# A two-layer attention and MLP kernel: pairwise LayerNorm rstd, zeroing and warming by TensorE, split weight loads, activations stored with chunks innermost, and an offset table for the planner

## Chip, cores, metric

The kernel runs on one core of a Trainium2 chip (trn2). Times are device microseconds of that core. A comparison uses fast runs only, and a ratio is of runs made on the same chip in the same rounds (e1, the last run, has one run of the kernel before of its own; the other seven are those of the runs d1 to d4, on the same chip). Runs whose labels start with a, b and c were made on three different chips, d and e on a fourth, so where ratios of different letters are set side by side, each was taken against the kernel before on its own chip.

The granted clock is the share of TensorE's full clock that its throttle let through; 1.00 is full speed. PE is the matmul engine (TensorE), PEld its weight loads, DVE VectorE, ACT ScalarE, POOL GpSimd, SP the engine that issues DMAs.

## The reference, cut

```python
# x: 1 x 2048 x 512 bf16.  Two layers, each:
x = x + A(layernorm(x))     # 32 heads of 16, causal window of 256, projections wqkv and wo
x = x + B(layernorm(x))     # gelu(x @ w1 + b1) @ w2 + b2, hidden size 1792
def _layernorm(x, eps=1e-5):
    return (x - mean(x)) / sqrt(var(x) + eps)
```

## The kernel before

A planner inside the kernel schedules its operations by list scheduling, with a priority and an estimated duration for each, and emits one fixed order for each engine. Semaphores hold the dependences. An engine can come to stand at an operation whose input is late: in d1, below, DVE stood 4.80 us at a copy whose input had not landed, with other work behind it. An operation may have an alternative engine, and the planner chooses at its planned time.

LayerNorm of a tile of 128 tokens gives `xn` (tokens on partitions). PE transposes its four 128-column chunks to PSUM (the memory that PE writes its results to), and DVE or ACT copies the transposed tile to `xnTA` (for Q, K, V) or `xnTB` (for the MLP). Q, K and W1 read those as the moving operand (the one that streams through the array), V as the stationary one (the weights).

```python
xnTA = sb("xnTA", [P, 2, DC, 2 * P])        # P = 128, DC = 4: chunk, then token
xnTB = sb("xnTB", [P, 2, DC, 4 * P])
...                                         # start
for h in range(2):                          # DVE zeroes PSUM
    add("dve", lambda e, B, h=h: e.memset(ps[:, 4 * h : 4 * h + 4, :], 0.0), 2200, ...)
...                                         # layernorm(tau, layer, dst, dcol, dname, prio), for one tile
add("dve", ... e.bn_stats(...) ...); add("dve", ... e.bn_aggr(...) ...)
add("pool", ... veps = var + EPS, 215, ...); add("pool", ... rstd = pow(veps, -0.5), 590, ...)
add("dve", lambda e, B: e.tensor_scalar(out=xn[:, s, :], in0=X[:, t, :], scalar1=mean, scalar2=rstd,
    op0=ALU.subtract, op1=ALU.mult), 310, ...)
add("pe", tr, 4 * 56.0, ...)                # four transposes to PSUM
evac(lambda B: dst[:, :, dcol : dcol + P],  # DVE or ACT: tokens adjoin in memory
     lambda B: psb[:, B[g][0], 0 : DC * P].rearrange("p (c q) -> p c q", c=DC), 512, ...)
...                                         # uses
(Wqkv_sb[:, dc, ...], xnTA[:, xs, dc, :], ...)                     # Q, K: stationary, moving
(xnTA[:, xs, dc, j * P : (j + 1) * P], Wqkv_sb[:, dc, 2 * D : 3 * D], ...)   # V
(W1_sb[:, dc, fc * P : (fc + 1) * P], xnTB[:, js, dc, 0:M], ...)   # W1, M = 512 or 256
```

The softmax here doesn't subtract the row's maximum and nothing guards it: scores larger than these inputs give would overflow.

## Time and profile before

The median was 534.04 us in the first three runs.

| | before |
|---|---|
| span of the profiled run | 535.7 us |
| PE, ACT, DVE, POOL busy | 472.1, 427.4, 387.3, 292.4 us |
| first exponential | 20.64 us |
| 20 W1 matmuls of 512 columns in a row | 4.49 us |

The page's first part, of the kernel before:

```profile
span 535.7 us, 19845 instructions
## 1 busy us (share of the span) xinstructions
PE 472.1 (88%) x8944; PEld 254.8 (48%) x8944; DVE 387.3 (72%) x739; ACT 427.4 (80%) x514; POOL 292.4 (55%) x376
```

Busy time in windows, kernel before. Each line is a stretch, its length, busy time and instructions of PE, PEld, DVE, ACT and POOL, then granted clock, DMA share and GB/s:

```profile
0.00:20.00 20.00, 9.50 (x68) 6.60 (x68) 13.07 (x25) 5.46 (x8) 10.74 (x46) 1.00 0.94 313
20.00:80.00 60.00, 45.29 (x1100) 26.65 (x1100) 49.22 (x99) 51.04 (x60) 40.28 (x52) 0.89 0.18 46
80.00:500.00 420.00, 385.05 (x7511) 201.63 (x7510) 313.98 (x596) 357.67 (x418) 235.92 (x273) 0.96 0.06 14
```

Groups of instructions, kernel before (output and inputs, shapes, count, then busy us and mean ns of one, then idle before it):

```profile
L585 PE MATMUL ps<-xnTB,W_sb 128*128 128x512 bf16 x336 | 82.1, 385 | 4.7 <-ACT gT L829 2.3 <-DVE gT L817 0.9 <-DVE xnTA L538 0.6
...
L585 PE MATMUL ps<-xnTA,Wqkv_sb 128*128 128x256 bf16 x512 | 71.4, 283 | 8.8 <-DVE KT L629 2.7 <-ACT E L704 1.9 <-ACT QT L540 1.4
...
L561 DVE TENSOR_SCALAR xn<-X,statmv,rstd 128x512 bf16<-128x512 bf16 x64 | 41.5, 653 | 2.7 <-POOL rstd L558 2.5
...
L540 ACT ACTIVATE xnTB<-ps 128x512 bf16<-128x512 bf16 x14 | 8.4, 613 | 1.6 <-PE ps L569 1.4
...
L538 DVE COPY xnTB<-ps 128x512 bf16<-128x512 bf16 x18 | 7.5, 422 | 7.0 <-PE ps L569 6.9
```

### The profile page before, as it was taken

The numbers are of one execution on the slowest core, as the hardware profiler recorded it, in microseconds if no ns is written. First come the engines' busy times: TensorE is split into PE (matmuls) and PEld (weight loads), VectorE is DVE, ScalarE is ACT, GpSimd is POOL, SyncE is SP. The second block draws the span as 40 slices with busy tenths as digits, with TensorE's granted clock in tenths as the row PEclk, the third lists the DMA queues.
The fourth block names the chain that finished last, engine by engine and source line by source line (L and its number), as shares of the span: only waits on it lengthen the run. The fifth ranks groups of instructions, "written<-read, shape, count | busy, mean of one in ns | idle before, by whom it ended". The sixth has DMA issues, their size and how long they took to land.

```text
span 535.7 us, 19845 instructions
## 1 busy us (share of the span) xinstructions
PE 472.1 (88%) x8944; PEld 254.8 (48%) x8944; DVE 387.3 (72%) x739; ACT 427.4 (80%) x514; POOL 292.4 (55%) x376
## 2 busy tenths in 40 slices
PE   3886688998979999599999879998999879989997
PEld 2543455555544545345444444444544444444563
DVE  5996878496979578775899588884878648793531
ACT  2689779888987988979888988689876888699552
POOL 6576746274684457452588347860585425871410
PEclk9997979999979999689999999999999989999999
DMA  8910001010100001000000011000110001100000
GB/s 277 325 42 23 2 4 23 1 25 1 24 2 13 12 3 23 4 1 22 14 13 3 2 23 23 2 4 6 33 29 21 2 8 39 42 2 4 29 21 29
DMA packets 16020, 15.82 MB, mean 30 GB/s; under 512 B 3264, under 2 KB 15424, under 8 KB 15936
## 3 DMA queue, kind: packets, MB, share of 16 engines
q1 hardware_dynamic: 15936, 14.56, 9.5%
q8 instruction: 70, 1.15, 0.9%
q14 instruction: 14, 0.11, 0.1%
HBM read 8.00 MB, written 2.10 MB: 19 GB/s over the span
## 4 chain that ended last, share of the span: by engine, by line
PE 60%; DVE 18%; ACT 18%; issue 2%; POOL 2%; POOLq 0%; DVEq 0%
PE ps L585 46%; ACT E L704 12%; PE ps L737 6%; PE ps L691 6%; DVE KT L629 3%; DVE xn L561 2%; DVE stat L551 2%; ACT gT L820 2%; DVE E L715 2%; PE ps L569 2%; DVE OD L747 2%; DVE gT L817 1%; ACT L820 1%; DVE X L841 1%; DVE X L594 1%
## 5 line engine op out<-in xcount | busy, mean ns | idle before, releaser
L704 ACT ACTIVATE E<-ps 128x1024 bf16<-128x1024 f32 x320 | 305.5, 1037 | 58.8 <-PE ps L691 58.1
L718 POOL TENSOR_TENSOR E<-E,mask 128x512 bf16<-128x512 bf16 x151 | 177.3, 1182 | 143.4 <-ACT E L704 143.1
L585 PE MATMUL ps<-xnTB,W_sb 128*128 128x512 bf16 (+1 forms) x560 | 116.8, 347 | 5.1 <-ACT gT L829 2.3
L585 PE MATMUL ps<-W_sb,gT 128*128 128x512 bf16 x448 | 114.9, 380 | 0.3 <-DVE X L841 0.3
L715 DVE TENSOR_TENSOR E<-E,mask 128x512 bf16<-128x512 bf16 x105 | 66.0, 632 | 27.0 <-ACT E L704 26.8
L691 PE MATMUL ps<-QT,KT 32*64 32x320 bf16 (+4 forms) x3072 | 70.2, 267 | 14.8 <-ACT E L704 8.5
L585 PE MATMUL ps<-xnTA,Wqkv_sb 128*128 128x256 bf16 x512 | 71.4, 283 | 8.8 <-DVE KT L629 2.7
L585 PEld LDWEIGHTS ps<-xnTB,W_sb 128*128 128x128 bf16 x560 | 51.9, 101 | 49.4 <-issue 3.9
L691 PEld LDWEIGHTS ps<-QT,KT 32*64 32x64 bf16 x3072 | 34.3, 105 | 68.6 <-ACT E L704 33.5
L829 ACT ACTIVATE gT<-ps,b1T 128x512 bf16<-128x512 f32 (+1 forms) x92 | 50.2, 584 | 18.0 <-PE ps L585 17.7
L837 POOL TENSOR_TENSOR Xb<-X,b2all 128x512 f32<-128x512 bf16 x32 | 37.7, 1179 | 44.3 <-DVE X L841 29.8
L585 PEld LDWEIGHTS ps<-W_sb,gT 128*128 128x128 bf16 x448 | 39.9, 98 | 41.6 <-issue 3.6
L585 PEld LDWEIGHTS ps<-xnTA,Wqkv_sb 128*128 128x128 bf16 x512 | 46.6, 101 | 25.3 <-DVE KT L629 4.1
L747 DVE STREAM_TRANSPOSE OD<-ps 128x512 f32<-128x512 f32 x64 | 45.4, 710 | 17.2 <-PE ps L737 15.7
L737 PE MATMUL ps<-E,Va 64*17 64x64 bf16 (+3 forms) x1920 | 51.0, 240 | 5.8 <-ACT E L704 3.0
L737 PEld LDWEIGHTS ps<-E,Va 64*17 64x17 bf16 x1920 | 40.8, 89 | 27.9 <-issue 16.8
L737 PE MATMUL ps<-E,Vs 64*17 64x64 bf16 (+3 forms) x1920 | 51.7, 240 | 0.0
L629 DVE TENSOR_TENSOR KT<-ps,parmask 128x1024 bf16<-128x1024 f32 x32 | 38.4, 1208 | 17.7 <-PE ps L585 17.3
L841 DVE TENSOR_TENSOR X<-Xb,ps 128x512 bf16<-128x512 f32 x32 | 21.8, 681 | 34.1 <-PE ps L585 33.9
L569 PE MATMUL ps<-ident,xn 128*128 128x128 bf16 x256 | 25.9, 230 | 20.3 <-DVE xn L561 9.8
L561 DVE TENSOR_SCALAR xn<-X,statmv,rstd 128x512 bf16<-128x512 bf16 x64 | 41.5, 653 | 2.7 <-POOL rstd L558 2.5
L551 DVE BATCH_NORM_STATS2 stat<-X 128x6 f32<-128x512 bf16 x64 | 42.2, 665 | 0.4
(45 smaller groups left out, 481.7 us busy)
## 6 DMA issues: line engine op xcount, KB each, us to landing
Vs<-Va SPq DMA_DIRECT2D x64, 68.0 KB, 2.0
W_sb<-in_B_w_dram SPq DMA_DIRECT2D x2, 1792.0 KB, 14.8
out_dram<-X SPq DMA_DIRECT2D x16, 128.0 KB, 1.7
Wqkv_sb<-in_A_wqkv_dram SPq DMA_DIRECT2D x3, 512.0 KB, 7.0
X<-in_A_x_dram SPq DMA_DIRECT2D x1, 1024.0 KB, 10.4
X<-in_A_x_dram SPq DMA_DIRECT2D x2, 256.0 KB, 3.0
X<-in_A_x_dram SPq DMA_DIRECT2D x1, 512.0 KB, 8.4
Wo_sb<-in_A_wo_dram SPq DMA_DIRECT2D x1, 512.0 KB, 9.4
```

The source lines that it names most:

```text
L551: add("dve", lambda e, B: e.bn_stats(stat6[:, k6, :], X[:, t, :]), 680, reads=["X%d" % t], writes=["st%d" % k6], prio=prio)
L561: add("dve", lambda e, B: e.tensor_scalar(out=xn[:, s, :], in0=X[:, t, :], scalar1=statmv[:, k, 0:1], scalar2=rstd[:, k : k + 1], op0=ALU. ...
L585: r = e.matmul(ps[:, B[g][0], cols], lhsT, rhs, start=st, stop=sp)
L629: add("dve", lambda e, B, g=g, i=i: e.tensor_tensor(out=KT[:, kb, :, 2 * i : 2 * i + 2, :].rearrange("p a c q -> p a (c q)"), in0=ps[:, B[ ...
L691: x = e.matmul(ps[HK * par : HK * par + HK, bk[r], o : o + n], KT[rows, kb, par, c, m * HK : m * HK + HK], QT[rows, c, q : q + n], start=T ...
L704: a = (add("act", lambda e, B, g_=g_, gi=gi: e.activation(E[:, 2 * gi : 2 * gi + 2, e0 : e0 + 512], ps[:, B[g_][0] : B[g_][0] + 2, :], AF. ...
L715: add("dve", lambda e, B: e.tensor_tensor(out=Ew, in0=Ew, in1=Mw, op=ALU.mult), 355 * n, reads=["E%d%s" % (es, x) for es in ess for x in " ...
L718: alt=(("pool", lambda e, B: e.tensor_tensor(out=Ew, in0=Ew, in1=Mw, op=ALU.mult), POOL_M * n, POOL_H, True),))
L737: x = e.matmul(ps[32 * r : 32 * r + VW, B[g][par], q_lo * HK : q_hi * HK], V[rows, (2 * b + m // 2) % VR, c * HC + 2 * r + par, :], E[rows ...
L747: add("dve", lambda e, B: e.transpose(OD[:, s, :], ps[:, B[g][0] : B[g][0] + 2, 0 : 2 * P]), 715, reads=["ps:" + g], writes=["OD%d" % s], ...
L829: gelu_last[0] = add("act", lambda e, B, g=g, fc=fc: e.activation(gT[:, fc, 0:M], ps[:, B[g][0], 0:M], AF.Gelu_apprx_tanh, bias=b1T[:, fc ...
L837: add("pool", lambda e, B, t=tau % T, xs=xs: e.tensor_tensor(out=Xb[:, xs, :], in0=X[:, t, :], in1=b2all[:], op=ALU.add), 1180, reads=["X% ...
```

## The change

The intent is to start sooner, to take work off POOL and to fill PE's gaps with a better order:
- LayerNorm's rstd for two tiles at once, the add of eps on POOL or DVE, the normalisation on DVE or POOL.
- PSUM is zeroed by 18 zero matmuls, which also warm PE; the parity mask is made by three operations instead of 16 selects.
- Q and K weights are loaded in halves.
- Transposed activations are stored token first, the four chunks innermost.
- `_TUNE` holds an offset to the priority of nearly every operation, and a second one for its alternative engine, the outcome of a search. Planned durations are set anew.

```diff
+_TUNE = { "ln": [-704, -709, -762, ...], ... }     # [cut: 2584 numbers under 36 keys]
 def add(..., key=None, more=False):
+    if key in self.tune: prio += self.tune[key][j]   # [cut: counting j; alternatives take key + "*"]
-        xnTA = sb("xnTA", [P, 2, DC, 2 * P])
-        xnTB = sb("xnTB", [P, 2, DC, 4 * P])
+        xnTA = sb("xnTA", [P, 2, 2 * P, DC])
+        xnTB = sb("xnTB", [P, 2, 4 * P, DC])
-        for h in range(2):
-            add("dve", lambda e, B, h=h: e.memset(ps[:, 4 * h : 4 * h + 4, :], 0.0), 2200, ...)
+        for h in range(NWARM):                          # NWARM = 18
+            add("pe", lambda e, B, bk=bk: e.matmul(ps[:, bk, :], gT[:, 0, 0:P], gT[:, 0, :], ...), mm(512), ...)
+        load_w(0, 0, D // 2, ...); load_w(1, 0, D // 2, ...)   # [cut] Q and K in halves, then V
+            add("pool", addeps, 215, ..., alt=(("dve", addeps, 105, 0.0, False),))
+            add("pool", ... rstd[:, k : k + 2] = pow(rstd[:, k : k + 2], -0.5), 580, ...)
-            add("dve", <normalise>, 310, ...)
+            add("dve", norm, 395, ..., alt=(("pool", norm, POOL_XN, 0.0, True),))   # POOL_XN = 620.0
-            evac(lambda B: dst[:, :, dcol : dcol + P],
+            evac(lambda B: dst[:, dcol : dcol + P, :].rearrange("p q c -> p c q"),
-  xnTA[:, xs, dc, :]    xnTA[:, xs, dc, j * P : (j + 1) * P]    xnTB[:, js, dc, 0:M]
+  xnTA[:, xs, :, dc]    xnTA[:, xs, j * P : (j + 1) * P, dc]    xnTB[:, js, 0:M, dc]
```

## The prediction

> **What bounds the kernel now.** No engine alone. The page: PE 472.1 us busy of 535.7 (88%), ACT 427.4 (80%), DVE 387.3, POOL 292.4. The chain of waits is 60% PE, 18% ACT, 18% DVE: engines with fixed orders wait for each other in short pieces. By stretch (busy time in windows):
> - 0 to 20 us: PE 9.5 us busy; first transpose at 8.3 us, first projection at 10.5, first exponential at 20.6.
> - 20 to 80: PE 45.3, ACT 51.0 of 60, granted clock 0.89; no MLP work yet.
> - 80 to 500: PE 385 of 420 (35 us idle), clock 0.96.
> - 500 to 536: PE 32.2 of 36; the last 28 W2 matmuls run at 222 ns each.
>
> PE idles 63 us in all, and granted clock lost about 4% (some 22 us). The wait list gives PE's idle time to many releasers of 1 to 10 us each: poor ordering, not one slow operation. ACT waits 58 us for scores.
>
> **What the change does.**
> 1. *Start.* Two DVE memsets of PSUM (1.76 us each, until 5.19) go; the first statistics started at 5.11 although X was issued at 0.79 and landed about 3.0 us later: up to 1 us gained. 18 zero matmuls warm PE: the first 16 projection matmuls took 3.19 us, later groups of 16 took 1.91, so about 1.3 us.  Waiting for both tiles' statistics costs about 0.8 us. Half-size weight loads let K start earlier. Net 3 to 5 us.
> 2. *Paired rstd.* 64 pow (596 ns) and 64 add-eps (252 ns) become 32 each: about 27 us off POOL. Perhaps 1 to 3 us of time. POOL may now take normalisations, and DVE's mean of 653 ns for them (median 414, longest 1345) shows port waits that better placement can cut.
> 3. *Chunks innermost.* The evacuation writes with an 8-byte step. The Trainium skill, "VectorE: DVE Perf Modes", Mode 2×_1P, asks for unit step; so I expect DVE's copies of transposes to go from about 0.41 us to about 0.68 us (what its fp32 casts of this shape take): about 10 us more DVE work over 38 copies, mostly hidden. Matmuls read with the 8-byte step: two elements per 16-byte line, which "SBUF — State Buffer", the cachelines note under Door 1, gives as enough for full bandwidth. I expect W1 and projection matmul durations unchanged (379 and 273 ns). No trace shows that yet.
> 4. *Offset table.* Reorders every engine and reassigns alternatives. This is the main term: I expect it to remove about half of the 35 us idle in the middle plus part of the lost clock (20 to 24 us), and 4 to 6 us of 20 to 80.
>
> PE's work is unchanged, so busy time with full clock (about 450 us) plus start and drain is a floor near 470.
>
> **Prediction: 506 us**, 8 in 10 within 489 to 523. Faster by over 2%: 0.88; within 2%: 0.09; slower: 0.03.
>
> **What would show it.** First exponential by 16 to 17 us; PE busy share over 91%; clock at least 0.97; PE idle from 80 us on under 20 us; ACT waiting under 40 us for scores; POOL pow x32 at about 580 ns; transposes' DVE copies about 0.68 us.
>
> **What would make it wrong.** Strided moving or stationary reads slowing PE (durations of W1 and projection groups rise); a table tuned to planned durations that the chip doesn't keep, so idle moves instead of going; slower evacuations on the chain; warm-up lost because PE idles again.

## More of the kernel before

The mean of a matmul is its latency (385 ns for 512 columns), and neighbours overlap. What a matmul costs a busy PE is its spacing, which the timeline shows where a run of equal matmuls is unbroken. Here, 20 of 512 columns take 4.49 us, 225 ns each. That stretch runs to the end of the last one; from start to start it is (4.49 - 0.385) / 19 us, or 216 ns:

```profile
237.25 4.49 PE L585 MATMUL ps<-xnTB,W_sb 128*128 128x512 bf16 x20
```

## The result and the profile after

The changed kernel took 686.5 us (median of 4) against 534.75 for the kernel before: ratio 1.2837, interval 1.2806 to 1.2869. It is 28% slower where 5% faster was predicted.

The page's first part, changed kernel:

```profile
span 684.2 us, 19714 instructions
## 1 busy us (share of the span) xinstructions
PE 613.4 (90%) x8864; PEld 270.8 (40%) x8962; DVE 411.4 (60%) x753; ACT 439.5 (64%) x498; POOL 330.2 (48%) x299
```

The span grew by 148.5 us and PE's busy time by 141.3. PE's idle time grew by only 7 us, and PE's share of the span rose from 88% to 90%. By itself a high share says little; here it says that the same work takes PE longer.

Windows, changed kernel:

```profile
0.00:20.00 20.00, 16.39 (x70) 7.53 (x71) 9.45 (x25) 7.96 (x8) 12.05 (x24) 1.00 0.92 317
20.00:80.00 60.00, 49.43 (x865) 23.74 (x867) 38.60 (x68) 43.38 (x47) 35.40 (x30) 0.91 0.16 44
80.00:500.00 420.00, 381.07 (x5790) 168.16 (x5856) 274.23 (x499) 280.67 (x313) 219.10 (x192) 0.98 0.04 10
```

Between 80 and 500 us PE is as busy as before (381 against 385 us), at a slightly higher granted clock (0.98), and gets through 5790 instructions instead of 7511. The groups say which:

```profile
L841 PE MATMUL ps<-xnTB,W_sb 128*128 128x512 bf16 x316 | 152.8, 629 | 12.2 <-issue 5.1 <-DVE xnTB L779 2.9 <-ACT xnTB L781 2.3
...
L841 PE MATMUL ps<-xnTA,Wqkv_sb 128*128 128x256 bf16 x512 | 128.0, 404 | 5.6 <-ACT xnTA L781 1.8 <-DVE xnTA L779 1.6 <-ACT xnTB L781 0.7
...
L841 PE MATMUL ps<-W_sb,gT 128*128 128x512 bf16 x408 | 105.0, 381 | 5.8 <-issue 3.3 <-DVE xnTB L779 1.0 <-ACT gT L1076 0.6
...
L814 POOL TENSOR_SCALAR xn<-X,statmv,rstd 128x512 bf16<-128x512 bf16 x37 | 78.6, 2128 | 12.8 <-PE ps L825 10.8
...
L779 DVE COPY xnTB<-ps 128x512 bf16<-128x512 bf16 x23 | 29.8, 1303 | 29.4 <-PE ps L825 29.3
...
L781 ACT ACTIVATE xnTB<-ps 128x512 bf16<-128x512 bf16 x9 | 11.8, 1310 | 10.0 <-PE ps L825 10.0
```

Matmuls that stream `xnTA` or `xnTB` went from 385 to 629 ns and from 283 to 404; those of W2, which stream `W_sb`, stayed at 381. (Some records of matmuls are missing: 316 and 408 stand for 336 and 448.) The copies of transposes tripled on DVE and doubled on ACT. A normalisation on POOL, planned at 620 ns, takes 2128. The spacing, from the timeline of the changed kernel, to hold against 4.49 us:

```profile
295.91 9.20 PE L841 MATMUL ps<-xnTB,W_sb 128*128 128x512 bf16 x20
```

That is 460 ns a matmul instead of 225 (from start to start, 451 instead of 216). For 256 columns the timelines show 16 in 3.79 us after (237 ns each) and 14 in 1.70 us before (121). An estimate of the cost is 336 x 235 ns + (224 + 512) x 116 ns = 164 us, enough for the whole loss. It has three rivals: the slow copies, the offset table with its mis-planned normalisations, and both.

### The profile page after: what moved, and what is told of

Read it like the earlier page. It is cut to its first block, busy times and chain, and to the rows that moved or that the text cites. A ratio compares the mean times of both kernels' runs of the same rounds, so it can differ in the third digit from the quotient of the medians.

```text
span 684.2 us, 19714 instructions
## 1 busy us (share of the span) xinstructions
PE 613.4 (90%) x8864; PEld 270.8 (40%) x8962; DVE 411.4 (60%) x753; ACT 439.5 (64%) x498; POOL 330.2 (48%) x299
## 4 chain that ended last, share of the span: by engine, by line
PE 77%; DVE 13%; ACT 5%; issue 3%; POOL 1%; POOLq 0%
PE ps L841 63%; PE ps L947 6%; PE ps L993 5%; DVE xnTA L779 2%; ACT E L960 2%; DVE xnTB L779 1%; ACT xnTA L781 1%; PE ps L825 1%; DVE KT L885 1%; DVE OD L1003 1%; ACT xnTB L781 1%; PE ps L738 1%; DVE X L851 1%; DVE E L971 1%; DVE stat L791 1%
## 5 line engine op out<-in xcount | busy, mean ns | idle before, releaser
L960 ACT ACTIVATE E<-ps 128x1024 bf16<-128x1024 f32 x320 | 308.7, 1030 | 121.8 <-PE ps L947 121.6
L974 POOL TENSOR_TENSOR E<-E,mask 128x512 bf16<-128x512 bf16 x144 | 169.6, 1184 | 146.9 <-ACT E L960 146.6
L841 PE MATMUL ps<-xnTB,W_sb 128*128 128x512 bf16 (+1 forms) x540 | 208.2, 536 | 13.2 <-issue 5.2
L841 PE MATMUL ps<-xnTA,Wqkv_sb 128*128 128x256 bf16 x512 | 128.0, 404 | 5.6 <-ACT xnTA L781 1.8
L841 PE MATMUL ps<-W_sb,gT 128*128 128x512 bf16 x408 | 105.0, 381 | 5.8 <-issue 3.3
L841 PEld LDWEIGHTS ps<-xnTB,W_sb 128*128 128x128 bf16 x560 | 58.7, 111 | 110.5 <-issue 71.3
L814 POOL TENSOR_SCALAR xn<-X,statmv,rstd 128x512 bf16<-128x512 bf16 x37 | 78.6, 2128 | 12.8 <-PE ps L825 10.8
L947 PE MATMUL ps<-QT,KT 32*64 32x320 bf16 (+4 forms) x3072 | 70.6, 268 | 14.4 <-ACT E L960 7.6
L841 PEld LDWEIGHTS ps<-xnTA,Wqkv_sb 128*128 128x128 bf16 x512 | 53.3, 112 | 62.3 <-issue 7.7
L1073 DVE TENSOR_SCALAR gT<-ps,b1T 128x512 bf16<-128x512 f32 (+1 forms) x48 | 32.7, 682 | 40.7 <-PE ps L841 40.6
L779 DVE COPY xnTB<-ps 128x512 bf16<-128x512 bf16 x23 | 29.8, 1303 | 29.4 <-PE ps L825 29.3
```

Source lines behind the costliest of these rows:

```text
L779: return add("dve", lambda e, B: e.tensor_copy(dst(B), src(B)), 410 if two else d_psum(n), reads=reads, writes=writes + ([] if free else r ...
L814: return e.tensor_scalar(out=xn[:, s, :], in0=X[:, t, :], scalar1=statmv[:, k, 0:1], scalar2=rstd[:, k : k + 1], op0=ALU.subtract, op1=ALU ...
L841: r = e.matmul(ps[:, B[g][0], cols], lhsT, rhs, start=st, stop=sp)
L947: x = e.matmul(ps[HK * par : HK * par + HK, bk[r], o : o + n], KT[rows, kb, par, c, m * HK : m * HK + HK], QT[rows, c, q : q + n], start=T ...
L960: a = (add("act", lambda e, B, g_=g_, gi=gi: e.activation(E[:, 2 * gi : 2 * gi + 2, e0 : e0 + 512], ps[:, B[g_][0] : B[g_][0] + 2, :], AF. ...
L974: alt=(("pool", lambda e, B: e.tensor_tensor(out=Ew, in0=Ew, in1=Mw, op=ALU.mult), POOL_M * n, POOL_H, True),))
```

## The experiments

### The layout, taken out and put in

*a1_after_old_layout*: the change with the old layout, with the same order on every engine.

```diff
-        xnTA = sb("xnTA", [P, 2, 2 * P, DC])     # xnTB, its writes and its reads likewise
+        xnTA = sb("xnTA", [P, 2, DC, 2 * P])
```

> The whole change, but with the transposed activations in the layout of before (chunk outermost, tokens contiguous); the order on every engine is the same as in the changed kernel. Theory L (the layout costs the time): matmuls on these activations return to spacings of about 216 ns (512 columns) and 108 ns (256), copies of transposes to about 410 ns on DVE and 600 on ACT, and the time falls from 686 to 505 to 525 us, below before (534). Rival O (the offset table made an order for durations the chip does not keep, above all normalisations planned at 620 ns on POOL and measured at 2083): the time stays above 600 us.

Measured: 523.4 us, ratio to before 0.9754 (0.9693 to 0.9816), matmuls back at 380 and 279 ns. Rival O falls as a cause of the loss: the same order that took 686 us is now 2.5% faster than before. By the interval it is faster, though not surely by 2%.

*a2_before_new_layout*: the kernel before with the new layout alone.

> The kernel before with only the layout changed to chunks innermost, order unchanged. Theory L: 680 to 705 us (534 plus about 167 us of PE streaming: 336 matmuls at +239 ns, 224 and 512 at about +117, with little absorbed). Rival O: below 570 us.

Measured: 701.5 us, ratio 1.3074 (1.3007 to 1.3142). So the layout accounts for the whole loss, and the rest of the change is a gain.

### Reading or writing

In both, the plan is that of the kernel before. Their outputs are wrong, which doesn't matter for the times.

```diff
 # a3_before_read_strided: written as before, read with the 8-byte step
-    xnTB[:, js, dc, 0:M]
+    flat(xnTB)[0 : 4 * M].rearrange("p (q c) -> p c q", c=DC)[:, dc]
 # a4_before_write_strided: written with the 8-byte step, read as before
-    evac(lambda B: dst[:, :, dcol : dcol + P], ...)
+    evac(lambda B: flat(dst)[0 : 4 * M].rearrange("p (q c) -> p c q", c=DC)[:, :, dcol : dcol + P], ...)
```

> The kernel before; activations are written contiguous as before, but the matmuls read them with the 8-byte step (wrong results on purpose). Theory L with the matmul read as its cause: 670 to 700 us, copies of transposes unchanged at about 410 and 600 ns. Rival E (the slow strided evacuation copies, 1300 ns on DVE and ACT, sit on the chain and cost most of it): below 570 us.

> The kernel before; activations are written with the 8-byte step, but the matmuls read contiguous (wrong results on purpose). Theory L with the matmul read as its cause: 540 to 560 us, only the copies at about 1300 ns show (about 34 us more DVE and 18 us more ACT work, partly hidden). Rival E: above 620 us.

Measured: reading alone 676.6 us, ratio 1.2613 (1.2550 to 1.2676); writing alone 568.0 us, ratio 1.0593 (1.0529 to 1.0657). Both expectations named the right side, but writing cost more than the 540 to 560 us given. Together (1.3074) they cost almost the sum, 26.1% and 5.9%. In the groups of the strided writes (a4), the copies are slow:

```profile
L567 DVE COPY xnTB<-ps 128x512 bf16<-128x512 bf16 x18 | 23.2, 1302 | 8.8 <-PE ps L598 8.7
...
L569 ACT ACTIVATE xnTB<-ps 128x512 bf16<-128x512 bf16 x14 | 18.3, 1336 | 3.5 <-PE ps L598 3.5
```

Of the 164 us estimated for reading, 139 (676.6 less the 537.7 of before in those rounds) show in the time: PE's busy time grew by 154 us (472.1 to 626.2), and its idle time shrank by 15. The strided copies add latency between a transpose and the matmuls that wait for it. PE's waits for these copies, all lines together, are 4.9 us in the kernel before and 24.5 us in a4. That is 20 of the 30 us that it lost, although neither DVE (72% busy) nor ACT (79%) is full. One of these lines, projections that wait for a copy on DVE, in the kernel before and in a4 (us in total, times, longest):

```profile
PE ps L585 <- DVE xnTA L538: 0.6, 2, 0.3
```

```profile
PE ps L614 <- DVE xnTA L567: 8.5, 12, 1.2
```

### Which step is slow

*b1_before_pairs_innermost* stores two chunks innermost, so the step is 4 bytes. *b2_before_read_16byte_step* reads the layout with chunks innermost as even tokens, then odd ones.

```diff
+    flat.rearrange("p (h q t) -> p h t q", h=2, t=2)      # b1: 4-byte step, written and read, result right
+    flat.rearrange("p (b a c) -> p c a b", a=2, c=DC)     # b2: 16-byte step in Q, K, W1 reads, result wrong
```

> The kernel before with two chunks innermost, so that the matmuls read every second element (a 4-byte step[...]) and the evacuations write with that step; results stay right. Theory S (the moving operand streams at full rate only where neighbouring elements adjoin): spacing of the 512-column matmuls about 450 ns as with the 8-byte step, time near 700 us. Rival C (the rate [...]falls off at some step): spacing about 216 ns, time below 575 us.

> The kernel before with chunks innermost, where the matmuls read even tokens first and then odd ones, so with a 16-byte step[...] (wrong results on purpose). Theory S (only adjoining elements stream at full rate, otherwise one element per slow cycle): same spacing as with the 8-byte step, about 455 ns, time 695 to 710 us. Rival C[...]: about 900 ns, time above 850 us.

Measured in one look each: 547.4 and 1070.1 us. The timeline lines of the two, in that order:

```profile
240.94 4.69 PE L614 MATMUL ps<-xnTB,W_sb 128*128 128x512 bf16 x20
```

```profile
445.89 18.16 PE L614 MATMUL ps<-xnTB,W_sb 128*128 128x512 bf16 x20
```

| step between elements | 2 B | 4 B | 8 B | 16 B |
|---|---|---|---|---|
| 20 matmuls of 512 columns, us | 4.49 | 4.69 | 9.20 | 18.16 |
| ns each | 225 | 235 | 460 | 908 |
| ns from start to start | 216 | 226 | 451 | 899 |
| granted clock in that stretch | 1.00 | 1.00 | 1.00 | 0.50 |
| DVE copy with that step in the write, median ns | 424 | 735 | 1307 | not tried |
| ACT copy likewise, median ns | 597 | 748 | 1308 | not tried |

Rival C holds. Theory S expected 450 ns at 4 bytes, and it got 235. But the 16-byte stretch ran at a granted clock of 0.50 (the mean of b2 is 0.67), and a stretch at 450 ns slowed to half by the clock would look the same. The trace of b2 settles it. In a stretch at full clock the matmuls are just as far apart, (5.56 - 1.08) / 5 us, or 896 ns. The stretch at full clock, then the windows of it and of the 18.16 us:

```profile
430.66 5.56 PE L614 MATMUL ps<-xnTB,W_sb 128*128 128x512 bf16 x6
```

```profile
430.66:436.00 5.34, 5.34 (x14) 0.57 (x6) 2.66 (x5) 1.94 (x2) 1.98 (x2) 1.00 0.01 3
446.00:464.00 18.00, 18.00 (x22) 2.56 (x22) 3.32 (x7) 3.38 (x4) 0.79 (x2) 0.50 0.00 1
```

The 8-byte step doesn't follow the clock either: in the changed kernel 18 matmuls of 256 columns took 4.24 us (from 153.55 us on) at a mean granted clock of 0.60, and 16 took 3.79 us at 1.00, 226 ns from start to start in both. Without a step the clock counts: in the kernel before, 15 took 3.27 us at 0.54, and 14 took 1.70 us at 1.00.

So in these runs a moving operand of bf16 streams at nearly full rate at a step of 4 bytes, and at a rate that halves with each further doubling, whatever the granted clock. That b2 was granted so little clock, though PE was busy for 93% of its span, is not explained by any run. As a stationary operand the 8-byte step is cheap: in the changed kernel V's weight loads took 117 ns on average instead of 97, and V's matmuls kept a median of 379 ns. (Even that rise need not be the step's: loads of W1's weights, whose layout did not change, rose from 101 to 111 ns.) What in the memory makes it so no run here shows.

### What the rest of the change brought

The prediction gave the whole change 28 us and let the layout cost next to nothing; the rest brought 2.5%, some 13 us. These runs use the old layout.

```diff
 # b3_oldlayout_norm_on_DVE
-    add("dve", norm, 395, ..., alt=(("pool", norm, POOL_XN, 0.0, True),))
+    add("dve", norm, 395, ...)
 # b4_oldlayout_norm_DVE_no_offsets: b3 and, as c3_oldlayout_no_offsets without b3:
-    }, _TUNE)
+    }, {})
```

> The whole change with the old layout, and with the normalisation never given to POOL (27 of 64 were on DVE, 37 on POOL at 2.1 us each against a planned 0.62). Theory N (that mis-sized alternative eats the expected gain: PE waited 11 us for it, and 16 us of weight-load waits): 508 to 516 us, against 523 with it. Rival T (the order itself is what stays short of the gain): 519 to 528 us.

> As the run before it (old layout, normalisation on DVE), with every offset of the table at zero. If the table is the main term of the gain, as predicted: 528 to 540 us. If the table brings nothing on the chip: the same as the run before it within 1%.

> The whole change with the old layout, POOL still free to take normalisations, all offsets of the table zero. If the table is worth what the prediction gave it (20 us and more): above 540 us. If the table brings little on the chip: 524 to 532 us.

| ratio to before | with the table | without |
|---|---|---|
| normalisation on DVE or POOL | 0.9754 (a1) | 1.0143 (c3: 1.0079 to 1.0206) |
| normalisation on DVE only | 0.9886 (b3: 0.9842 to 0.9929) | 0.9851 (b4: 0.9801 to 0.9900) |

The table is worth 3.8% (some 21 us: medians 523.4 and 544.5) in the plan it was searched for, and nothing once another set of alternatives makes the planner choose another order (531.0 us for b3, 529.2 for b4). Without the table, letting POOL normalise costs 3%. So b3 could not size the normalisations, because it also threw away the order. Its 531.0 us missed the 508 to 516 of Theory N, and lies past the rival's 528 too.

*d2_oldlayout_norms_moved_to_DVE* separates the two: the plan is left as it is, and the 37 normalisations then run on DVE at their planned places.

```diff
         order = PL.run()
         B = PL.gmap
+        for i in order:
+            if PL.nodes[i]["key"][0] == "xn":
+                PL.nodes[i]["eng"] = "dve"
```

> The whole change with the old layout; the plan is made as before, and then each of the 37 normalisations planned on POOL is put on DVE at its planned time, so that the order of PE, ACT and of everything else stays. Theory N (the 2.1 us normalisations on POOL cost what PE waits for them, 11 us): 510 to 516 us. Rival T (DVE has no room, 37 more at 0.41 us delay what PE waits for): 520 to 530 us.

Measured: 517.5 us, ratio 0.9604 (0.9541 to 0.9668), against 0.9754 with POOL. Theory N holds in kind, though the time lies just outside the range named. In a1 PE waited 11.1 us for POOL's normalisations; in d2 it waits for none, as they are all on DVE. POOL was also freed for other work: PE's waits for its masks fell from 3.6 to 1.0 us, and no run tells the two apart. The line of a1:

```profile
PE ps L825 <- POOL xn L814: 11.1, 12, 1.5
```

*c4_late_weights_true_norm_cost* told the planner the true 2083 ns instead:

> The kernel of the first run of this group, with the planner told that a normalisation on POOL takes 2083 ns instead of 620. Theory N (POOL's slow normalisations cost time where PE waits for them, 11 us in all): 508 to 515 us. Rival T (the offsets were searched with 620 ns, and any other order loses more than the normalisations cost): 518 to 530 us, as the run with normalisation on DVE suggests.

Measured: 542.7 us, ratio 1.0123 (1.0057 to 1.0188), worse than a1 and b3 and outside what either theory gave. After b3 it is the second time that a changed plan lost what the table had found; it also carries c1's edit (below), which by itself cost about 1%.

### The start: a gain handed on from wait to wait

In a1 the first exponential started at 16.46 us, 4.2 us sooner than before (20.64), as predicted. The timeline of a1 shows where that went (start, length, engine, instructions, and in brackets the idle time before and what ended it):

```profile
31.71 0.39 PE L993 MATMUL ps<-E,Va 64*17 64x256 bf16 x4 [3.51 <-DMA Vs<-Va]
...
32.37 1.89 PE L841 MATMUL ps<-xnTA,Wqkv_sb 128*128 128x256 bf16 x8
...
34.91 1.94 ACT L960 ACTIVATE E<-ps 128x1024 bf16<-128x1024 f32 x2 [5.98 <-PE ps L947]
```

The first product with V waited 3.5 us for a shifted copy of V (`Vs`). After that PE ran at half speed for a while: 8 matmuls took 1.89 us at a granted clock of 0.50, where 8 take 1.05 us at 1.00 (d1, below). ACT idled 6 us. The plan gives each copy of V 2.2 us, but here the longest took 7.2 us to land, queued behind the loads of W1 and W2, which nothing needs before the MLP starts (at 70.6 us in the kernel before).

```diff
 # c1, c2: after planning, in the DMA queue only
+    late = loads of W1, W2, b1 and b2;  order = order without late
+    at = position after the 4th copy of V;  order[at:at] = late      # d1, d3: after the 8th
 # e1: as d3, with b1 left where it was
```

> The whole change with the old layout, and with only the order of the DMA queue changed: the loads of W1, W2 and the two biases are issued after the first four shifted copies of V instead of before them. Theory D (the start's gain is given back because PE waits 3.5 us, cold afterwards, for copies of V queued behind 3.6 MB of weights that nobody needs before 70 us): the first product with V starts by 26 us instead of 31.7, ACT's 6 us wait there goes, time 515 to 519 us against 523. Rival: the same within 2 us, because another wait takes its place.

> The kernel before with the same change of the DMA queue's order. Theory D: in it the first product with V started at 29.8 us with PE idle only 0.2 us, so it gains less: 532 to 537 us against 537. Rival (the queue was as costly there): 525 to 530 us.

Measured: 529.0 us (0.9858, 0.9805 to 0.9912) and 543.3 us (1.0132, 1.0070 to 1.0194). c2 is slower than the kernel before. c1 is about 1% slower than a1, with intervals that just overlap, on another chip. The edit was wrong: copies that the first product needs came after the fourth and were now behind the weights. In c1's timeline:

```profile
36.33 0.39 PE L993 MATMUL ps<-E,Va 64*17 64x256 bf16 x4 [7.98 <-DMA Vs<-Va]
```

> The whole change with the old layout; W1, W2 and the biases are loaded after the first eight shifted copies of V (the first product with V needs more than the first four: in the run that put the weights after four it waited 8 us). Order of the compute engines unchanged. Theory D (the start's gain is lost to the queue): first product with V by 28 us instead of 31.7, no wait of PE for a DMA there, 516 to 520 us against 523. Rival: within 2 us of 523.

> Both edits of the two runs before this together. If each theory holds and they add: 504 to 512 us. If neither: 520 to 530 us.

Measured: d1 525.3 us (0.9767, 0.9707 to 0.9826), no gain; d3 514.6 us (0.9560, 0.9502 to 0.9619), not clearly better than d2. Yet the wait was gone: in d1 the first product starts at 28.17. A new one stood behind it, in d1's timeline:

```profile
28.17 0.28 PE L993 MATMUL ps<-E,Va 64*17 64x256 bf16 x4
...
28.56 1.05 PE L841 MATMUL ps<-xnTA,Wqkv_sb 128*128 128x256 bf16 x8
...
41.11 0.86 DVE L775 CAST b1T<-b1raw 128x14 f32<-128x14 bf16 x1 [4.80 <-DMA b1raw<-in_B_b_dram]
...
43.40 1.46 PE L841 MATMUL ps<-xnTA,Wqkv_sb 128*128 128x256 bf16 x6 [5.42 <-DVE QT L779]
```

The copy of a small bias, planned early on DVE because DVE had room, stood at the head of DVE's queue while its load, moved back with the weights, was still on its way. PE stood behind DVE.

> The run with both edits, with the load of the first bias left in front of the copies of V: only W1, W2 and the second bias wait for the first eight copies. In the run with both edits DVE stood still for 4.2 us for that bias (in a copy that had been planned early), PE 4.8 us behind it. Theory D in full (the start's gain is passed from one wait to the next, and is kept once the last of them is gone): no such waits of PE before 45 us, 507 to 512 us against 514.6. Rival (yet another wait takes its place): 513 to 516 us.

Measured: 508.45 us (6 runs, 508.14 to 508.84), ratio 0.9447 (0.9401 to 0.9493), results right. It was run at another time. Leaving this one load in front took d3's 514.6 to 508.5, and the intervals of the ratios don't overlap. In e1's timeline the first product with V starts at 25.67 us and PE has no wait over 0.9 us before 45 us but for the 1.2 us ahead of its first zero matmul:

```profile
25.67 0.28 PE L993 MATMUL ps<-E,Va 64*17 64x256 bf16 x4
```

This is the fastest kernel, 5.5% faster than before. Which of its waits is next in line was not followed.

*d4_oldlayout_warmup_8*: 8 zero matmuls instead of 18.

> The whole change with the old layout, with 8 zero matmuls instead of 18 (each bank zeroed once, no further warming). If the warming is worth what the prediction gave it: 1 to 2 us slower than 523. If the first projections run cold only because their inputs come late: the same within 1 us.

Measured: 522.3 us, ratio 0.9701 (0.9635 to 0.9767); a1 had 0.9754 with an overlapping interval, so no end-to-end effect is seen. Its effect at the start is plain all the same. First projections in the timeline, d4 (granted clock 0.50) and then a1 (1.00):

```profile
10.64 3.62 PE L841 MATMUL ps<-xnTA,Wqkv_sb 128*128 128x256 bf16 x16
```

```profile
10.43 1.98 PE L841 MATMUL ps<-xnTA,Wqkv_sb 128*128 128x256 bf16 x16
```

Warming brings the first exponential from 18.50 to 16.46 us. Both kernels then wait for the same copy of V (first product at 31.17 and 31.71), and there the 2 us end. What warming is worth once that wait is gone was not run.

## Why the prediction was wrong, point by point

- **The step that failed** is the second half of point 3: "I expect W1 and projection matmul durations unchanged (379 and 273 ns)". They became 629 and 405 ns (medians), and their spacing doubled, from 216 to 451 ns for 512 columns; read alone with that step, the kernel before lost 26% (a3). The prediction rested on a note on cachelines in the Trainium skill, "SBUF — State Buffer", under Door 1, that two hits to a 16-byte line give full bandwidth. The runs differ: 8 bytes, two elements to a line, is half rate; 4 bytes, four to a line, is nearly full. The measurement decides. The prediction did name this among what would make it wrong, but gave slower a chance of only 3%. The page's sentence is about the memory in general, no trace had shown a strided moving operand, and 1072 matmuls (336 + 224 + 512) depended on it.
- **Slower evacuations**: right in kind, mis-sized. DVE's copies were to go to 0.68 us and took 1.30; ACT's were not expected to change and went from 0.6 to 1.3. They cost the kernel before 5.9% alone (a4), not "mostly hidden". "VectorE: DVE Perf Modes", Mode 2x_1P, asks for unit step, and the rise from 0.424 to 0.735 us at a 4-byte step agrees with the loss of that mode; that 8 bytes cost almost twice as much again is not in it.
- **The table**: right in kind, mis-sized. In the plan it was made for it is worth 3.8% (21 us) against the same kernel without it. But that kernel (c3) is 1.4% slower than the kernel before, against which 20 to 24 us were predicted in the middle and 4 to 6 more ahead of it; against the kernel before, all of the change but the layout brought some 13 us. PE's share from 80 to 490 us was 94% in a1, against 92% from 80 to 500 us before.
- **POOL may take normalisations**: expected to help and cost instead. POOL takes 2.1 us where DVE takes 0.41; moving the 37 back in place gained 1.5%.
- **The start**: the first exponential came at 16.46 us with the old layout, in the predicted 16 to 17, and the warm-up was worth its 1.3 us and more there. That this would become 3 to 5 us of time failed. It was handed to a wait for a DMA. In the changed kernel itself the first exponential came at 21.59 us, because the layout slowed the copies and projections ahead of it.
- **Pairing**: pow x32 as predicted, at 717 ns on average instead of about 580. Its own share of the time was not run, nor that of the half loads and of the parity mask.

With the layout put back, the normalisations on DVE and the DMA queue reordered (e1), the kernel takes 508 us, near the 506 predicted. That agreement is luck: the predicted kernel took 686 us, and the prediction knew nothing of the layout's cost or of the two repairs.

## What to carry to other kernels

Before a layout is changed, ask for every reader and writer what step between neighbouring elements it will see, and measure that step on the moving operand of a matmul by itself; one look would have shown this loss. When PE's busy time grows and its instruction count doesn't, look for a longer spacing before looking at the order. A searched order is worth only as much as the durations and the plan it was searched with: repair the execution in place rather than re-plan, and follow a gain at the start until it reaches the end, because a fixed order hands it to the next wait.

## What the Trainium skill lacked or had wrong

- "SBUF — State Buffer", Door 1, cachelines: it says that two or more hits to a 16-byte line give full bandwidth, and lists 8 bf16 elements as how far one can stride for free. For a bf16 moving operand of a matmul the runs show 216, 226, 451 and 899 ns from start to start for 512 columns at steps of 2, 4, 8 and 16 bytes: two elements to a line is half rate, and 8 bf16 a quarter.
- "TensorE: Matmul & The Clock Gate" gives the spacing of matmuls by columns and clock alone, and no step of the moving operand. With an 8-byte step 256 columns took 226 ns at mean granted clocks of 0.60 and 1.00 alike. The same step in V's stationary operand cost little: weight loads at 117 instead of 97 ns. No page says that the granted clock can be low while PE streams with a wide step: in b2, from 436.5 to 490 us, PE was busy for 53.27 of 53.50 us at a granted clock of 0.50.
- "VectorE: DVE Perf Modes", Mode 1x, gives one result per cycle for any stride. A copy of 128x512 bf16 from PSUM takes 424, 735 and 1307 ns at steps of 2, 4 and 8 bytes in the output: the second is compatible with it, the third is not, since the step alone nearly doubles the time. Slow writes of words that don't adjoin are measured in "Vector Engine (DVE) Microarchitecture Reference", Measured stream behaviour on trn2, but for 4-byte types only; no page has the 2-byte outputs of this case. For ACT the runs show 597, 748 and 1308 ns; "ScalarE: Activation LUTs" gives no cost of a strided write.
- "GPSIMD Engine Reference", key points, calls DVE about twice as fast for elementwise work, and the page's measurement of it is an fp32 add of two tensors. For the normalisation (tensor_scalar with two per-partition scalars, 128x512 bf16) POOL took 2083 ns and DVE 413 (medians), five times.
